# Attention on one core: another order of scores, products and normalisation in the steps, and other due times for the work beside them

## The chip, the core and the metric

One core of a Trainium2 chip runs the whole program. The metric is device time in microseconds of one execution; lower is better. Engines are called as the profile calls them: PE (TensorE, matmuls), PEld (its weight loads), DVE (VectorE), ACT (ScalarE), POOL (GpSimd), SP (SyncE, which issues the DMAs that matter here). Each works through its own instructions in order and waits on semaphores of the others.

## The reference

Three stages in a row: an attention, a dense layer pair with a rational activation, and eight experts of which each token takes one. The change lies in the first. Its mathematics, per batch (4), head (8), with 576 rows and 64 columns in float32:

```python
scores = (q @ k.T) / 8
thresh = scores.max(-1) - tau            # tau = 0.02
scores = where(scores >= thresh, scores, -1e9)
attn = exp(scores - scores.max(-1))
attn = attn / (attn.sum(-1) + 1e-9)
x = attn @ v
```

The result x, transposed and split into a float16 high and low part, is the input of the dense layers.

## The kernel before, in words

The attention (function `attention`, lines 161 to 631) handles two batches together (a batch pair, bp) and two heads together (a pair of heads, group g). A unit u is one head of a batch pair: nine tiles of 128 rows (t = 0 to 8), the middle one (t = 4) made of half a tile of each batch. There are N = 144 steps i, nine per unit, 18 per group, in eight groups; LAG = 12 more steps drain. The loop at line 596 writes out, for each step i, the instructions of all engines in this order:

- S(i+1), `emit_s`: the scores of the next tile, PE, float32, into one of three PSUM tiles of `ps_s` (line 377). q carries the factor -1/8, so the largest score is a minimum.
- the products with v of tile i - 12, `emit_pv` (lines 446 to 469): fourteen float16 matmuls of 65 columns with transposed weights `pt` and v in a high and a low part `vh`, `vl` (the 65th column, ones, gives the row sums). They add up in `xps`, a PSUM tile with two halves of three tiles of rows each; every third step a matmul of `tiny` (line 455; one row in 128 columns) starts a half.
- `emit_e`: the row's minimum (DVE, line 393) and the exponential (ACT, line 395) into a buffer e of four.
- `emit_thr`: minimum plus tau, by ACT or DVE as `THR` says (lines 402, 404).
- `emit_p(i-1)`: one DVE instruction compares with the threshold and multiplies (line 410), and is the last reader of that score tile; ACT rounds to float16 (line 419), POOL computes the remainder (lines 421, 422), and after every second step SP issues one transposing DMA from the ring `php` of four into `pt` (line 425). Steps from `DIRECT` = 138 on go through PE transposes (`emit_t`, line 431) instead.
- every third step, `emit_x`: reciprocal of the sums (line 486) and the multiply (line 488), both DVE, from the half of `xps` just finished into `xf`. In such a step S(i+1) is written behind the products.
- whatever `PLAN` has due at this step, through the dictionary `plan` filled by `at`. From step 112 on the next stage's generator `tail` advances too; its decoding of weights on DVE begins near step 144.

`PLAN` (line 138) gives steps within a group for the work beside the chain: loads of the next q and k (`load_qk`, SP), turning of q and k on PE in pieces of 16 matmuls or one (`piece_t`, line 244) and their copies by ACT (`piece_out`, lines 259 to 270), loads of v for the second batch pair (`load_v`), its sums (`sum_v1`), the split of v (`hi_v` on ACT, `lo_v` on POOL), and `emit_xt`: three PE transposes of `xf` (line 496), ACT's rounding to the high part of `xT` (line 498), DVE's low part (line 499). q, k and x share one PSUM bank, `tp`, for being turned. `FIRST` does the first group's q and k.

Of the kernel before, what the change touches and what calls it, by code (L numbers as in the profile page):

```python
# [18 lines left out]
P = 128  # L19
# [67 lines left out]
def plan_decode():  # L87
# [63 lines left out]
}  # L151
X_LAG = 0
THR = 'svvvsvvvv'
# [7 lines left out]
def attention(nc, tc, q, k, v, tau, xT, vs, ident, tail):  # L161
# [17 lines left out]
    e_p = pool(early, "e", 4)  # L179
# [20 lines left out]
    tiny = fix.tile([1, P + 3 * D1], BF16, name="tiny")  # L200
# [115 lines left out]
    def row_ps(bp, n):  # L316

        if bp == 0:
            return xps.rearrange("p a b c -> p (a b c)")[:, 2 * P + P * n:3 * P + n]
        return ps_x.tile([P, 4, P], F32, tag="tp", name="tp")[:, 0, 0:(P, 1)[n]]  # L320
# [23 lines left out]
    def hi_v(g, hh):  # L344
        bp, hp = divmod(g, 4)
        src = vall[:, hp, bp, hh, 0:8]
        nc.scalar.activation(vh[:, g % 2, hh, 0:8, 0:D], src, AF.Copy, scale=vs[:, bp, 0:1])
        if hh:
            nc.scalar.activation(last_v(g, vh), last_v(g), AF.Copy, scale=vs[:, bp, 0:1])

    def lo_v(g, a):
# [3 lines left out]
        parts = [(vall[:, hp, bp, hh, ts], *(x[:, g % 2, hh, ts, 0:D] for x in (vh, vl)))]  # L355
        if a == 3:
            last = last_v(g), last_v(g, vh), last_v(g, vl)
            parts += [tuple(x[:, :, h] for x in last) for h in range(2)] if g == 0 else [last]
# [113 lines left out]
    rs = [None]  # L472

    def emit_x(u, tg, part):
        xo = xps[:, (3 * u + tg) % 2]
        if part == 0:
            if tg == 0 and u % 2 == 0:
                xfs[u // 2] = x_p.tile([P, UT, 2, D], F32, tag="xf", name="xf")
            rs[0] = sm.tile([P, 3, 1], F32, tag="rinv", name="rinv")
            tot = xo[:, :, D:D1]  # L480
            i = u * UT + 3 * tg
            if i + 2 >= DIRECT:
                nc.vector.tensor_tensor(
                    rs[0], tot, sums[:, i - N + 3 * UT:i + 3 - N + 3 * UT].rearrange("p (a b) -> p a b", b=1), op=ALU.add)
                tot = rs[0]
            nc.vector.reciprocal(rs[0], tot)
        else:
            nc.vector.tensor_tensor(
                xfs[u // 2][:, 3 * tg:3 * tg + 3, u % 2], xo[:, :, 0:D], rs[0].to_broadcast([P, 3, D]), op=ALU.mult)

    def emit_xt(g, tg):
        bp, hp = divmod(g, 4)
        t0 = 3 * tg
        tp = ps_x.tile([P, 4, P], F32, tag="tp", name="tp")[:, 0:3]
        for t in range(3):
            nc.tensor.transpose(tp[:, t], xfs[g][:, t0 + t].rearrange("p h d -> p (h d)"), ident)
# [19 lines left out]
    nc.vector.memset(tiny[:, 0:P], 2.0**-15)  # L516
    nc.vector.memset(tiny[:, P:], 0.0)
    nc.vector.memset(tiny[:, P:].rearrange("p (a b) -> p a b", b=D1)[:, :, D:D1], 1e-9 * 2.0**15)
# [39 lines left out]
    for a in range(4):  # L558
# [9 lines left out]
    for g in range(1, NG):  # L568
        s0 = (g - 1) * GT
        o = 3 if g == 1 else 0  # L570
# [7 lines left out]
        for n in range(3):  # L578
            for i, (ts, outs) in ((1, ("k_t", "k_out")), (0, ("q_t", "q_out"))):
                at(s0 + o + PLAN[ts][n], piece_t, g, i, PIECES[n])  # L580
                for hh in range(2):
                    at(s0 + o + PLAN[outs][2 * n + hh], piece_out, g, i, *PIECES[n], (hh,))
        for hh in range(2):
            at(s0 + PLAN["v_hi"][hh], hi_v, g, hh)
        for a in range(4):
            at(s0 + PLAN["v_lo"][a], lo_v, g, a)
    x_lag = lambda u: X_LAG if u < NU - 1 else 0
# [1289 lines left out]
```

## Time and profile before

| | us |
|---|---|
| median of 3 runs | 1077.81 (1077.54 to 1080.48) |
| the profiled execution | 1076.23 |
| its span, first to last instruction | 1074.3 |
| mean granted clock of TensorE | 0.968 of 2.4 GHz |

Of the span the attention takes the first third: the first matmul of the dense layers starts at 356.91 us, in PE's order behind the last turned output. In rows of a timeline the columns are start, duration, engine, line, operation, tiles written and read, count, and in brackets how long the engine had been idle before it and what ended that. In rows of stretches they are the stretch, its length, the busy time and the instructions of each engine, the granted clock as a share of 2.4 GHz, the mean busy share of the DMA engines and their GB/s. In rows of groups: busy time in us, mean ns of one, then the idle time in front of them.

### The profile page before, as it was taken

How to read it: one execution, taken by the hardware profiler on the slowest of the kernel's cores; microseconds unless marked ns; L12 is line 12 of the kernel's file. 1: busy time of each engine (PE TensorE's matmuls, PEld its weight loads, DVE VectorE, ACT ScalarE, POOL GpSimd, SP SyncE). 2: the span in 40 equal slices, each digit the busy share in tenths (PEclk: the TensorE clock that was granted, in tenths of full speed). 3: DMA queues.
4: the chain of work that ended last, by engine and by line, in shares of the span. 5: the costliest groups of instructions: out<-in, count | busy, mean ns of one | idle time of the engine just before them, and what ended most of it. 6: DMA issues, size and time to landing. Idle time of an engine off the chain costs nothing. (4 is left out here: it accounts for less than half of the span.)

```text
span 1074.3 us, 19863 instructions
## 1 busy us (share of the span) xinstructions
PE 972.9 (91%) x7377; PEld 729.1 (68%) x7377; DVE 826.3 (77%) x1406; ACT 700.0 (65%) x1055; POOL 508.2 (47%) x547
## 2 busy tenths in 40 slices
PE   7999999999897688888899999998988999999996
PEld 5676676676666455555566666665557799999995
DVE  3987788788787579999897787899896697665552
ACT  4987897887775278777776656666564454554552
POOL 3687787788760254545555444443534013211120
PEclk8999999999997699999999999999899999999998
DMA  9799998998992213323200312204132111111340
GB/s 218 139 202 195 197 186 156 181 167 153 214 173 79 80 59 117 98 70 93 84 1 1 85 63 60 60 30 127 31 89 81 48 50 50 59 41 40 99 138 23
DMA packets 227176, 108.42 MB, mean 101 GB/s; under 512 B 189824, under 2 KB 214400, under 8 KB 227072
## 3 DMA queue, kind: packets, MB, share of 16 engines
q1 hardware_dynamic: 223808, 97.12, 41.0%
q0 software_dynamic: 3120, 9.96, 2.8%
q8 instruction: 60, 0.98, 0.4%
q14 instruction: 44, 0.36, 0.1%
q10 hardware_dynamic: 144, 0.00, 0.0%
HBM read 82.61 MB, written 13.63 MB: 90 GB/s over the span
## 5 line engine op out<-in xcount | busy, mean ns | idle before, releaser
L939 PE MATMUL h<-xT,wih 128*128 128x384 f16 x768 | 194.3, 336 | 44.1 <-DVE s L956 31.8
L966 POOL TENSOR_TENSOR t<-t,ah 128x768 f32<-128x768 f32 x48 | 87.8, 1828 | 229.5 <-ACT t L965 214.7
L421 POOL TENSOR_TENSOR php<-e,php 128x512 f16<-128x512 f32 x138 | 160.3, 1162 | 73.0 <-ACT php L419 72.9
L377 PE MATMUL s<-kt,qz 128*128 128x288 f32 (+1 forms) x640 | 172.2, 426 | 13.4 <-DVE e L410 10.0
L939 PEld LDWEIGHTS <-wih 128*128 128x128 f16 x768 | 69.9, 100 | 110.6 <-DVE s L956 39.1
L395 ACT ACTIVATE e<-s,mn 128x576 f32<-128x576 f32 x144 | 106.5, 739 | 58.4 <-DVE mn L393 44.7
L1009 PE MATMUL acc<-woh,gh 128*128 128x512 f32 x288 | 126.5, 439 | 4.2 <-ACT part L1026 1.8
L939 PE MATMUL h<-xT,wil 128*128 128x384 f16 x384 | 128.4, 334 | 0.5 <-POOL wil L858 0.5
L377 PEld LDWEIGHTS s<-kt,qz 128*128 128x128 f32 (+1 forms) x640 | 99.0, 181 | 41.5 <-DVE e L410 13.2
L393 DVE TENSOR_REDUCE mn<-s 128x1 f32<-128x576 f32 x144 | 108.0, 750 | 24.6 <-PE s L377 24.3
L410 DVE SCALAR_TENSOR_TENSOR e<-s,mn,e 128x576 f32<-128x576 f32 x144 | 116.5, 809 | 5.4 <-ACT e L395 4.1
L1009 PE MATMUL acc<-wol,gh 128*128 128x512 f32 x288 | 114.9, 399 | 2.6 <-POOL wol L864 2.6
L1009 PE MATMUL acc<-woh,gl 128*128 128x512 f32 x288 | 114.4, 397 | 0.0
L1705 POOL DMA_INDIRECT out_dram<-os,sidx x19 | 23.8, 1253 | 182.2 <-ACT os L1704 152.9
L991 POOL TENSOR_TENSOR gl<-s,gh 128x768 fp32r<-128x768 f32 x48 | 91.3, 1903 | 6.9 <-issue 4.6
L419 ACT ACTIVATE php<-e 128x576 f16<-128x576 f32 x138 | 93.7, 679 | 0.2
L469 PEld LDWEIGHTS <-pt 128*128 128x128 f16 (+1 forms) x2142 | 76.4, 101 | 19.3 <-issue 9.2
L469 PE MATMUL xps<-vs__112,pt 128*128 128x65 f16 (+1 forms) x2142 | 86.4, 195 | 0.0
L963 ACT ACTIVATE ah<-h,cvs 128x768 f32<-128x768 f32 x48 | 43.3, 902 | 53.6 <-PE h L939 50.0
L975 ACT ACTIVATE h<-t,co 128x768 f32<-128x768 f32 x48 | 43.4, 905 | 52.1 <-DVE s L969 18.6
L1638 DVE TENSOR_TENSOR wol<-xT,woh 128x1024 fp32r<-128x1024 f32 x45 | 56.8, 1270 | 17.0 <-ACT woh L1637 17.0
L1009 PEld LDWEIGHTS acc<-woh,gh 128*128 128x128 f32 x288 | 54.8, 190 | 20.6 <-ACT part L1026 4.7
(401 smaller groups left out, 2341.7 us busy)
## 6 DMA issues: line engine op xcount, KB each, us to landing
xT<-in_moe_w_dram SPq DMA_DIRECT2D x80, 512.0 KB
raw<-in_moe_w_in_dram SPq DMA_DIRECT2D x16, 512.0 KB
raw<-in_moe_w_out_dram SPq DMA_DIRECT2D x16, 512.0 KB
yd<-y SPq DMA_DIRECT2D x18, 256.0 KB
raw<-in_k_dram SPq DMA_DIRECT2D x16, 256.0 KB
raw<-in_q_dram SPq DMA_DIRECT2D x16, 256.0 KB
xT<-in_v_dram SPq DMA_DIRECT2D x8, 512.0 KB
part<-part SPq DMA_DIRECT2D x15, 256.0 KB
```

Source lines behind the costliest of these rows:

```text
L377: nc.tensor.matmul(ps[po:po + m, half, 0:288], qz[:, g % 2, hh, t, qt:qt + m], kt[:, c:c + 288], start=True, stop=True)
L393: nc.vector.tensor_reduce(mn[:, 0:1], ps[:, :, 0:288], axis=AX.XY, op=ALU.min)
L395: nc.scalar.activation(e, ps[:, :, 0:288], AF.Exp, bias=mn[:, 0:1], scale=-1.0)
L410: nc.vector.scalar_tensor_tensor(e, ps[:, :, 0:288], mn[:, 1:2], e, op0=ALU.is_le, op1=ALU.mult, accum_out=sums[:, i - N + 3 * UT:][:, 0:1 ...
L419: nc.scalar.activation(ph.rearrange("p (a b) -> p a b", a=2), e, AF.Copy)
L421: nc.gpsimd.tensor_tensor(pl[:, 64:S], ef[:, 0:512], ph[:, 0:512], op=ALU.subtract)
L469: nc.tensor.matmul(x, w, y, start=False, stop=(t % 3 == 2 and n == len(seq) - 1))
L939: nc.tensor.matmul(hb[:, 0:n], w[:, k, fc * P:(fc + 1) * P], xT[:, k, t0:t0 + TR, lo, :], start=(i == 0), stop=(i == 11))
L966: nc.gpsimd.tensor_tensor(t1, t1, ah, op=ALU.mult)
L991: nc.gpsimd.tensor_tensor(gl, s, gh.bitcast(F32), op=ALU.subtract)
L1009: nc.tensor.matmul(acc[r, i], g[:, i * P:(i + 1) * P], w, start=first and m == 0, stop=last and m == 2)
L1638: (self.nc.gpsimd if pool else self.nc.vector).tensor_tensor(cut(lo), src, cut(hi).bitcast(F32), op=ALU.subtract)
```

## The change

In the loop, S(i+1) is written ahead of the products with v in every step. `emit_x` is one function for both of its parts; it is due one step later than before, three steps being those of a half of `xps`, and stands at the head of its step, ahead of the products, the minimum and the rest (in the very last step behind them). `emit_xt` keeps the transposes and the high part; the low part becomes `emit_xlo`, due one step later. The due times in `PLAN` change: pieces of k at steps -2, 0, 2 of a group, of q at 4, 6, 8, turned output at 10, 12, 14 (28, 30, 32 counted from its own group's start), copies of a piece at the step after it and both halves together; for the second group these come six steps later (`late`) where it was three. The loads of v for the second batch pair come at 14, 20, 26, 32 instead of 12, 20, 28, 40; the low parts of v in five steps instead of four, the last high part in a step of its own. The threshold is always DVE's. The buffers e become five. `tiny` has 128 rows, zero but for the first. The sums' row in the second batch pair uses a tile of `ps_s` instead of `tp`.

```diff
 PLAN = {
-    "k_load": (7, 9),
-    "q_load": (14, 16),
-    "k_t": (-1, 3, 4),
-    "k_out": (0, 1, 3, 3, 5, 6),
-    "q_t": (7, 10, 11),
-    "q_out": (8, 9, 10, 10, 12, 13),
-    "v_hi": (15, 17),
-    "v_lo": (15, 17, 19, 20),
+    "k_load": (4, 6),
+    "q_load": (10, 12),
+    "k_t": (-2, 0, 2),
+    "q_t": (4, 6, 8),
+    "late": 6,
+    "v_hi": (11, 13, 15),
+    "v_lo": (14, 17, 20, 23, 25),
     "v_first": (2, 7, 8),
-    "v_next": (12, 20, 28, 40),
-    "v_sum": (24, 29, 42, 60, 61, 62, 68, 69),
-    "xt": (32, 33, 34),
+    "v_next": (14, 20, 26, 32),
+    "v_sum": (25, 31, 37, 43, 45, 46, 48, 49),
+    "xt": (28, 30, 32),
 }
-THR = 'svvvsvvvv'
+THR = 'v'
-    e_p = pool(early, "e", 4)
+    e_p = pool(early, "e", 5)
-    tiny = fix.tile([1, P + 3 * D1], BF16, name="tiny")
+    tiny = fix.tile([P, P + 3 * D1], BF16, name="tiny")
...
     def emit_xt(g, tg):
...
-        hi, lo = (xT[:, hp, bp * UT + t0:bp * UT + t0 + 3, n] for n in range(2))
-        nc.scalar.activation(hi, tp, AF.Copy)
-        nc.vector.tensor_tensor(lo, tp, hi, op=ALU.subtract)
+        nc.scalar.activation(x_rows(g, tg, 0), tp, AF.Copy)
+        xts[g, tg] = tp
+
+    def emit_xlo(g, tg):
+        nc.vector.tensor_tensor(x_rows(g, tg, 1), xts.pop((g, tg)), x_rows(g, tg, 0), op=ALU.subtract)
...
-        o = 3 if g == 1 else 0
+        o = PLAN["late"] if g == 1 else 0
...
-            pre[u * UT + 3 * tg + 2 + LAG + x_lag(u)] = (u, tg)
+            pre[min(u * UT + 3 * tg + 3 + LAG, N + LAG - 1)] = (u, tg)
...
-        if i + 1 < N and not early_pv:
+        if i + 1 < N:
             emit_s(i + 1)
+        done = i in pre and i < N + LAG - 1
+        if done:
+            emit_x(*pre[i])
         if 0 <= i - LAG < N:
             emit_pv(i - LAG)
...
-        if i + 1 < N and early_pv:
-            emit_s(i + 1)
         if i < N:
             emit_e(i)
-        if i < N and THR[i % len(THR)] != "v":
-            emit_thr(i)
         if 0 <= i - 1 < N:
             emit_p(i - 1)
...
-        if last:
-            emit_x(*pre[i], 0)
-        if i < N and THR[i % len(THR)] == "v":
+        if i in pre and not done:
+            emit_x(*pre[i])
+        if i < N:
             emit_thr(i)
-        if last:
-            emit_x(*pre[i], 1)
```

## Rows read from the trace of the kernel before

**Rows 1.** The page's part 1: each engine's busy time over the span.
```profile
PE 972.9 (91%) x7377; PEld 729.1 (68%) x7377; DVE 826.3 (77%) x1406; ACT 700.0 (65%) x1055; POOL 508.2 (47%) x547
```
**Rows 2.** Stretches: six groups of 18 steps, from S(17) to S(125).
```profile
51.11:88.29 37.18, 35.67 (x445) 26.05 (x441) 30.48 (x63) 32.27 (x59) 30.76 (x46) 1.00 1.11 202
...
243.74:282.30 38.56, 36.23 (x442) 26.67 (x442) 31.42 (x66) 30.73 (x57) 30.77 (x46) 1.00 0.93 163
sum 231.19, PE 217.35 PEld 159.67 DVE 188.60 ACT 188.57 POOL 184.74; mean PE 36.23 PEld 26.61 DVE 31.43 ACT 31.43 POOL 30.79
```
**Rows 3.** Stretches: S(3) to S(6); S(125), S(139), S(143); the drain.
```profile
14.86:28.11 13.25, 8.53 (x63) 6.11 (x62) 6.04 (x10) 6.51 (x12) 3.98 (x6) 0.74 0.97 210
...
282.30:310.45 28.15, 25.76 (x292) 18.29 (x292) 23.95 (x52) 21.33 (x38) 24.28 (x37) 0.94 1.07 212
310.45:321.93 11.48, 9.39 (x100) 6.86 (x99) 7.93 (x20) 7.27 (x15) 3.56 (x6) 1.00 0.86 162
321.93:336.00 14.07, 9.15 (x152) 7.67 (x152) 11.12 (x31) 7.79 (x18) 0.00 (x0) 0.92 0.22 74
336.00:356.91 20.91, 18.88 (x84) 16.09 (x84) 11.73 (x33) 7.14 (x14) 2.38 (x2) 0.50 0.34 102
```
**Rows 4.** Timeline, all engines, around a step that turns output.
```profile
240.73 1.14 PE L377 MATMUL s<-kt,qz 128*128 128x288 f32 x4
...
241.74 0.56 DVE L499 TENSOR_TENSOR xT<-tp,xT 128x384 f16<-128x384 f32 x1 [1.09 <-ACT xT L498]
...
241.79 0.25 PE L455 MATMUL xps<-tiny 1*128 1x195 bf16 x1
...
241.98 0.60 PE L469 MATMUL xps<-vs__112,pt 128*128 128x65 f16 x14
242.21 0.75 DVE L393 TENSOR_REDUCE mn<-s 128x1 f32<-128x576 f32 x1
...
242.43 0.52 PE L496 MATMUL tp<-ident,xf 128*128 128x128 f32 x3
...
242.87 0.81 DVE L410 SCALAR_TENSOR_TENSOR e<-s,mn,e 128x576 f32<-128x576 f32 x1
...
243.74 1.24 PE L377 MATMUL s<-kt,qz 128*128 128x288 f32 x4 [0.79 <-DVE e L410]
```
**Rows 5.** Groups by line and form, 40 to 330 us: DVE's instructions of a step.
```profile
L410 DVE SCALAR_TENSOR_TENSOR e<-s,mn,e 128x576 f32<-128x576 f32 x135 | 109.3, 809 | 5.4 <-ACT e L395 4.1 <-ACT mn L402 0.6
L393 DVE TENSOR_REDUCE mn<-s 128x1 f32<-128x576 f32 x134 | 100.5, 750 | 13.9 <-PE s L377 13.8
...
L404 DVE TENSOR_SCALAR mn<-mn,tauc 128x1 f32<-128x1 f32 x105 | 20.5, 195 | 0.0
...
L488 DVE TENSOR_TENSOR xf<-xps,rinv 128x192 f32<-128x192 f32 x44 | 15.7, 357 | 0.0
...
L499 DVE TENSOR_TENSOR xT<-tp,xT 128x384 f16<-128x384 f32 x21 | 11.7, 557 | 28.1 <-ACT xT L498 28.1
...
L486 DVE RECIPROCAL rinv<-xps 128x3 f32<-128x3 f32 x44 | 7.6, 173 | 5.6 <-PE xps L469 5.6
```
**Rows 6.** Timeline, drain: DVE's multiply and the next matmul into xps.
```profile
330.67 0.36 DVE L488 TENSOR_TENSOR xf<-xps,rinv 128x192 f32<-128x192 f32 x1
...
331.08 0.24 PE L455 MATMUL xps<-tiny 1*128 1x195 bf16 x1 [1.00 <-DVE xf L488]
```
**Rows 7.** Timeline, start: the second group's first piece of k on PE.
```profile
22.29 1.97 PE L244 MATMUL tp<-ident,raw 128*64 128x128 f32 x16 [4.72 <-DMA raw<-in_k_dram]
```
**Rows 8.** Waits, 51.11 to 321.93 us: total, times, longest.
```profile
ACT e L395 <- POOL php L422: 12.6, 11, 2.1
```
**Rows 9.** Timeline, SP's queue: first, one between and the one after ten transposes.
```profile
57.12 2.74 SPq L425 DMA_TRANSPOSE pt<-php  x1
...
65.75 3.25 SPq L425 DMA_TRANSPOSE pt<-php  x1
...
101.40 3.31 SPq L425 DMA_TRANSPOSE pt<-php  x1
```

More of the change, by code (lines that the diff above doesn't have):

```diff
@@ L319, in row_ps @@
             return xps.rearrange("p a b c -> p (a b c)")[:, 2 * P + P * n:3 * P + n]
-        return ps_x.tile([P, 4, P], F32, tag="tp", name="tp")[:, 0, 0:(P, 1)[n]]
+        return ps_s.tile([P, 2, 512], F32, tag="s", name="s")[:, 0, 0:(P, 1)[n]]
     def red_row(bp):
@@ L354, in lo_v @@
         ts = slice(4 * half, 4 + 4 * half)
-        parts = [(vall[:, hp, bp, hh, ts], *(x[:, g % 2, hh, ts, 0:D] for x in (vh, vl)))]
-        if a == 3:
+        if a < 4:
+            parts = [(vall[:, hp, bp, hh, ts], *(x[:, g % 2, hh, ts, 0:D] for x in (vh, vl)))]
+        else:
             last = last_v(g), last_v(g, vh), last_v(g, vl)
-            parts += [tuple(x[:, :, h] for x in last) for h in range(2)] if g == 0 else [last]
+            parts = [tuple(x[:, :, h] for x in last) for h in range(2)] if g == 0 else [last]
         for src, hi, lo in parts:
@@ L471, in attention, with emit_x @@
     xfs = {}
-    rs = [None]
-    def emit_x(u, tg, part):
+    def emit_x(u, tg):
         xo = xps[:, (3 * u + tg) % 2]
[L476 to L487, printed above, removed]
-            nc.vector.tensor_tensor(
-                xfs[u // 2][:, 3 * tg:3 * tg + 3, u % 2], xo[:, :, 0:D], rs[0].to_broadcast([P, 3, D]), op=ALU.mult)
+        if tg == 0 and u % 2 == 0:
+            xfs[u // 2] = x_p.tile([P, UT, 2, D], F32, tag="xf", name="xf")
+        rs = sm.tile([P, 3, 1], F32, tag="rinv", name="rinv")
+        tot = xo[:, :, D:D1]
+        i = u * UT + 3 * tg
+        if i + 2 >= DIRECT:
+            nc.vector.tensor_tensor(
+                rs, tot, sums[:, i - N + 3 * UT:i + 3 - N + 3 * UT].rearrange("p (a b) -> p a b", b=1), op=ALU.add)
+            tot = rs
+        nc.vector.reciprocal(rs, tot)
+        nc.vector.tensor_tensor(
+            xfs[u // 2][:, 3 * tg:3 * tg + 3, u % 2], xo[:, :, 0:D], rs.to_broadcast([P, 3, D]), op=ALU.mult)
@@ L491, in emit_xt, with x_rows @@
+    def x_rows(g, tg, n):
+        bp, hp = divmod(g, 4)
+        t0 = bp * UT + 3 * tg
+        return xT[:, hp, t0:t0 + 3, n]
+    xts = {}
     def emit_xt(g, tg):
-        bp, hp = divmod(g, 4)
-        t0 = 3 * tg
         tp = ps_x.tile([P, 4, P], F32, tag="tp", name="tp")[:, 0:3]
         for t in range(3):
-            nc.tensor.transpose(tp[:, t], xfs[g][:, t0 + t].rearrange("p h d -> p (h d)"), ident)
-        hi, lo = (xT[:, hp, bp * UT + t0:bp * UT + t0 + 3, n] for n in range(2))
-        nc.scalar.activation(hi, tp, AF.Copy)
@@ L515, in attention @@
     nc.vector.memset(sums, 0.0)
-    nc.vector.memset(tiny[:, 0:P], 2.0**-15)
-    nc.vector.memset(tiny[:, P:], 0.0)
-    nc.vector.memset(tiny[:, P:].rearrange("p (a b) -> p a b", b=D1)[:, :, D:D1], 1e-9 * 2.0**15)
+    nc.vector.memset(tiny, 0.0)
+    nc.vector.memset(tiny[0:1, 0:P], 2.0**-15)
+    nc.vector.memset(tiny[0:1, P:].rearrange("p (a b) -> p a b", b=D1)[:, :, D:D1], 1e-9 * 2.0**15)
     nc.vector.memset(vl[:, :, :, :, D:D1], 0.0)
@@ L557, in attention @@
         at(PLAN["v_first"][1] + hh, hi_v, 0, hh)
-    for a in range(4):
+    at(PLAN["v_first"][1] + 1, hi_last, 0)
+    for a in range(5):
         at(PLAN["v_first"][2] + a // 2, lo_v, 0, a)
@@ L596, in attention @@
     while i < N + LAG or plan:
-        last = i in pre
-        early_pv = last and x_lag(pre[i][0]) == 0
         if DIRECT <= i - 2 < N - 1:
             emit_t(i - 2)
-        if i + 1 < N and not early_pv:
+        if i + 1 < N:
             emit_s(i + 1)
+        done = i in pre and i < N + LAG - 1
+        if done:
+            emit_x(*pre[i])
         if 0 <= i - LAG < N:
```

19 lines of the change are left out of this document (10 added, 9 removed).

## The prediction, written before the result was known

> **What bounds the kernel now.** I read the page's engine line first, then busy time by stretch, then one group's timeline, then durations by line. TensorE is busy 91% of the span [rows 1], but that is a mean over stages, and the change touches only the attention (start to 356.91 us) and its hand-over. So I cut the attention at starts of S, the scores' matmul, 18 steps (one pair of heads) apart: S(17) at 51.11, S(35) at 88.29 and so on to S(125) at 282.30. There are six such groups; the first, the last and the sum stand in [rows 2]. Read two columns: 231.19 us in all, PE busy 217.35. PE is the bound, yet idle for 13.84 us; DVE is busy 188.60, ACT 188.57, POOL 184.74, so none of them is a second bound on average. Nothing that keeps the same matmuls can win more than 13.84 us there. The other stretches [rows 3] are the start, where S(3) to S(6) take 13.25 us with PE busy 8.53; the last pair's steps (28.15 and 11.48 us with PE busy 25.76 and 9.39); and the drain from S(143), of which 336.00 to 356.91 runs at a granted clock of 0.50, the 1.2 GHz level.
>
> Where PE's idle time is made shows in [rows 4], a step that turns output for the next stage. DVE waited 1.09 us for ACT's rounding (L498) before it could write the low part (L499, 241.74). The next minimum (L393) is ready but stands behind it on DVE, then the product with the threshold (L410), and only that frees the score bank: S at 243.74 waited 0.79 us for it. S, minimum, exp, rounding, low part and S again run one after the other, with three such steps in a row in each group.
>
> **The change, part by part.**
>
> Turned output. The low part moves one step on, and the turns go from three consecutive steps to every second one. One L499 costs 0.557 us [rows 5] before and after; its wait goes, since ACT has rounded a step earlier. What is late next is PE itself, or the bank turn below.
>
> Output normalised one step on, S always ahead of the products with v. The reciprocal and the multiply (L486, L488) now stand ahead of the next minimum on DVE, and behind the end of the third product. Both halves of xps belong to one tile, and the trace shows them ordered against each other: the matmul of tiny into the other half began at 331.08, 0.05 us after the multiply (330.67 + 0.36) ended [rows 6]. So behind a waiting reciprocal are queued: the next minimum, the product L410, and through it S two steps on, and on PE the next products. From the end of the products: reciprocal and multiply 0.53 [rows 5], minimum to product 0.66, product 0.81 [rows 4, 5], and about 0.1 for the hand-overs, 2.1 us to the S that needs the bank. PE has meanwhile S 1.06, tiny 0.19 and the products 0.45 (starts 240.73, 241.79, 241.98, 242.43) [rows 4], 1.70 us, and any transposes placed in those two steps. Uncovered: 0.4 us for a turn without transposes. Of six turns a group, two have only a small tail transpose (about 0.14 us of cover), the other four a whole piece, turned output or the doubled scores of a middle tile. I put 0.55 us a group on turns and 0.25 on other short waits: 0.8 x 6 = 4.8 left of the 13.84, a gain of 9.0 us. Bounds: 13.84, and 3 if every turn loses 0.3 (36 x 0.3 = 10.8).
>
> The Trainium skill's page "PSUM — Partial Sum Buffer", section "PSUM bank collisions raise a hardware error", speaks against this move: accesses of two engines must be kept apart by bank and quadrant, not by address, so the second half doesn't let PE go on while DVE reads the first. The order at 331.08 agrees. By it tiny waits 0.55 us behind the turn, which the 1.06 us of S hides; by address alone it would wait for nothing, and the sum would be the same.
>
> Threshold always on DVE: four more a group at 0.195 [rows 5] make 0.8 us on a DVE busy 31.4 of 38.5 us [rows 2]; hidden, and ACT gets a little back. If DVE were the bound it would cost 5 us in all.
>
> Start. The first piece of the second pair's k is turned at step 4 in place of 2. PE, in order, waited 4.72 us for that load at 22.29 [rows 7], with S(4) to S(6) queued behind it; that is most of the 4.7 us of idle PE before S(6) [rows 3]. Two steps later, S(4), S(5) and the warming matmuls fill the wait: the piece still starts at 22.29, runs about 1.1, and S(6) starts near 23.4 in place of 28.11. Gain 4.7; at worst 2 if ACT's sums of v are next in line, at best 7, since the 0.74 clock of this stretch would rise with a fuller PE.
>
> Last pair. No q or k pieces are left to cover turns here. In 28.15 us PE is busy 25.76 at 0.94 clock; I give back about 1 us for the clock and take three uncovered turns of 0.4: 26.5, a gain of 1.6. In the 11.48 us after it, three turns of output with the wait of [rows 4] meet PE transposes of e; PE needs 9.39 [rows 3]; gain 2. Together 3.6, from 1 to 6.
>
> Drain. The decoding of weights on DVE is not changed. The normalisation now stands behind a step's decoding on DVE and can hold PE at three turns; PE's idle time just before 336, 14.07 less 9.15, bounds that at some +4. In return the low part's wait no longer blocks decoding. Were the clock to stay at 2.4 GHz, PE's 18.88 us from 336 would halve, and DVE's 11.73 [rows 3] would be the floor: -8. PE is as thinly used before it as now (9.15 of 14.07 us), so I take 0.
>
> tiny over 128 rows. 0.19 us from its start to the products' now; 195 columns at the pace of the products (0.45 / 14 for 65) take 0.10. Saves between 0 and 0.09 x 47 = 4.2; a load of 128 rows might cost 0.5 instead. I take 2, since the new form is the products' own.
>
> Fifth e buffer, low parts of v in five steps, both halves of a piece in one step: instruction counts stay; ACT's 12.6 us of waits for POOL [rows 8] lie beside a PE that is busy. Nothing. Without that cover it would be part of the 13.84 already counted.
>
> DMA. The loads of v for the second batch pair move from steps 12 to 40 into 14 to 32, on SP's queue among the transposes of the weights. In 57.12 to 101.40 this queue never rested: ten transposes with six loads of q or k and two of v in 44.28 us [rows 9]. A transpose alone takes 3.2 of the queue [rows 9], so 12 us are loads: about 1.1 for one of 256 KB and 2.7 for one of v with its tail. Steps 14 to 34 will ask for 10 x 3.2 + 6 x 1.1 + 4 x 2.7 = 49 us where PE needs 41. Eight us of lateness is about what the four-deep ring of php absorbs; I take +1, from 0 to +5.
>
> Sum: -4.7 - 9.0 - 3.6 + 0 - 2 + 1 = -18.3. The profiled execution took 1076.23 (span 1074.3), 1.6 below the median of 1077.81; set against the median it is 1059.5, against the execution 1057.9. I say **1059**.
>
> **Rivals.**
> - *The turn of the bank is the new wait.* DVE's order is for it, TensorE's cover against. If all 36 turns lose 0.4, 14.4 us replace the 13.84: no gain in the groups, 1068. Chance 0.14.
> - *The clock holds in the drain*: for it a denser end of the scores, against it the unchanged decoding. -8: 1051 and below. Chance 0.12.
> - *Slower: SP's queue sets the pace.* If lateness passes what ring and lag absorb, ACT waits to write php, and the chain runs at the queue's 4.43 us a pair. From S(17) to S(139), 61 pairs, 270 us against 259.3 now: +11, less 4.7 and 2 at both ends, +4: 1082. It decides if transposes start over some 8 us behind POOL beyond step 34. Against: after it a group asks only 9 x 3.2 + 4 x 1.1 = 33 us. The Trainium skill's page "DMA: Bandwidth & Descriptors", section "Issuing engines are not separate DMA queues", says that all issuers share the same sixteen engines; the busy queue here agrees, and no other queue would take these loads off. Chance 0.10.
> - *It does not do what it says*: one wait takes another's place on the same banks, and what the start gains is lost in the drain: 1075 to 1080. Chance 0.07.
>
> **How the numbers follow.** Forecast (1051 to 1067) 0.57. 0.3%, or 3.2 us, is about what a measurement here tells from no change. Faster 0.57 + 0.14 + 0.12 = 0.83, within 0.07, slower 0.10. The range takes in the clock's and the bank turn's cases, 1046 to 1073, and leaves out 0.17 and the last tails.
>
> **What would show it.** Right: waits of L499 for L498 near zero, S(17) near 46, groups of about 37 us with PE busy 36, S(6) near 23.4. The turn: S waiting for L410 in steps just behind a reciprocal. The queue: transposes starting 8 us behind POOL, ACT waiting at L419. Wrong at large: groups over 38.5 us, or a half-clock stretch longer than now.

## The result, and the profile after

The changed kernel takes 1065.6 us in the median of 7 runs (1062.79 to 1073.14), the kernel before 1077.81 (1077.12 to 1080.48): a ratio of 0.989 [0.986, 0.993], or 12.2 us less. The forecast was 1059 in a range of 1046 to 1073. The profiled execution took 1072.34 (span 1070.6), which is near the upper end of its seven. Nothing below rests on its total alone: the same kernel was profiled again (e1_again), and that execution took 1064.31.

Busy time by stretch of the kernel after, cut at the same starts of S as [rows 2] and [rows 3] (columns: stretch, its length, busy time and count on PE, PE's weight loads, DVE, ACT and POOL, granted clock, DMA share, GB/s): start to S(6), to S(17), the first three groups, the last group, the last pair's two pieces, the drain, and all that follows the attention.

```profile
0.00:23.77 23.77, 18.82 (x153) 13.37 (x153) 13.76 (x31) 13.45 (x22) 10.13 (x16) 1.00 1.00 224
23.77:46.49 22.72, 21.62 (x191) 15.49 (x189) 19.65 (x47) 19.59 (x34) 13.69 (x21) 1.00 0.88 157
46.49:83.63 37.14, 35.20 (x448) 27.12 (x444) 31.57 (x69) 32.98 (x57) 30.65 (x47) 1.00 1.08 205
83.63:128.49 44.86, 38.92 (x445) 29.29 (x446) 33.28 (x77) 34.10 (x59) 31.82 (x48) 0.92 1.09 200
128.49:164.78 36.29, 35.16 (x442) 27.12 (x442) 32.10 (x70) 30.45 (x52) 31.03 (x47) 1.00 1.00 172
...
237.34:273.62 36.28, 35.16 (x441) 27.13 (x442) 32.09 (x70) 30.45 (x52) 31.03 (x47) 1.00 1.09 184
273.62:299.29 25.67, 23.57 (x292) 18.07 (x292) 24.09 (x52) 19.47 (x31) 24.96 (x39) 1.00 1.20 216
299.29:311.12 11.83, 9.31 (x102) 6.80 (x99) 9.80 (x26) 6.78 (x15) 3.09 (x5) 1.00 0.83 155
311.12:344.74 33.62, 26.19 (x233) 22.97 (x233) 21.26 (x58) 14.09 (x31) 2.67 (x2) 0.67 0.31 95
344.74:1070.60 725.86, 654.21 (x3766) 492.51 (x3764) 555.96 (x807) 434.49 (x576) 267.36 (x191) 0.97 0.21 64
```

Set beside before: S(17) is 4.6 us earlier; the six groups take 227.1 in place of 231.19 (the last four 36.28 to 36.29 each, the last of them 38.56 before [rows 2], but the second 44.86); the last pair's 37.50 stands against 39.63, the drain's 33.62 against 34.98 [rows 3]. That makes 4.6 + 4.1 + 2.1 + 1.4 = 12.2 us, and the attention indeed ends at 344.74 in place of 356.91. Behind it this execution gave 8.5 us back (725.86 against 1074.3 - 356.91 = 717.39), at a mean granted clock of 0.97.

Two places carry the story. First the second group, which has a hole: a stretch in which the chain stands still. One wait of ACT in it (total, times, longest):

```profile
ACT php L419 <- DMA pt<-php: 4.6, 2, 4.1
```

The rows around the hole, each from its own engine's timeline (start, length, engine, line, what; in brackets the idle time before it and what ended it): POOL's end of one pair of php, the DMA transpose of this pair on SP's queue (its length there is that of the issue, not of the transfer), ACT's next write into the same buffer, and PE.

```profile
88.31 0.31 POOL L422 TENSOR_TENSOR php<-e,php 128x64 f16<-128x64 f32 x1
...
95.34 4.33 SPq L425 DMA_TRANSPOSE pt<-php  x1
...
103.27 0.68 ACT L419 ACTIVATE php<-e 128x576 f16<-128x576 f32 x1 [4.11 <-DMA pt<-php]
103.86 1.36 ACT L264 ACTIVATE qz<-tp,tauc 64x512 f32<-64x512 f32 x2
...
101.54 0.60 PE L469 MATMUL xps<-vs__112,pt 128*128 128x65 f16 x14
105.28 0.48 PE L237 MATMUL tp<-ident,tail 128*128 128x128 f32 x1 [3.14 <-ACT qz L264]
```

POOL had finished this pair at 88.62. SP's queue came to its transpose only at 95.34, 6.7 us late, and by the trace's semaphores the transpose landed at 103.19, 7.85 us after its start. Four pairs on, the ring of php comes round to the same buffer: ACT's write, ready 4.11 us earlier, began at 103.27. Behind it on ACT stood the copy of turned q (L264) that frees the tile of turns, and for that PE stood still from 102.14 to 105.28. From 104.4 to 111.2 the granted clock was at its lower level, 1.2 GHz, which is why the group's mean clock is 0.92.

The second place is a turn of the output bank in the last groups. Timeline, PE and DVE, around one reciprocal:

```profile
205.08 0.60 PE L469 MATMUL xps<-vs__112,pt 128*128 128x65 f16 x14
...
205.52 1.21 PE L377 MATMUL s<-kt,qz 128*128 128x288 f32 x4
205.72 0.18 DVE L483 RECIPROCAL rinv<-xps 128x3 f32<-128x3 f32 x1 [1.20 <-PE xps L469]
205.93 0.36 DVE L484 TENSOR_TENSOR xf<-xps,rinv 128x192 f32<-128x192 f32 x1
206.21 0.75 DVE L393 TENSOR_REDUCE mn<-s 128x1 f32<-128x576 f32 x1
...
206.57 0.25 PE L455 MATMUL xps<-tiny 128*128 128x195 bf16 x1
...
206.87 0.81 DVE L410 SCALAR_TENSOR_TENSOR e<-s,mn,e 128x576 f32<-128x576 f32 x1
...
207.74 1.24 PE L377 MATMUL s<-kt,qz 128*128 128x288 f32 x4 [0.34 <-DVE e L410]
```

DVE stood idle for 1.20 us until the products (L469) ended and it could take the reciprocal. From there the chain is the one of the forecast: 205.72 to 207.68 on DVE, and S waits 0.34 for the product L410 (0.4 was forecast). The wait of [rows 4], the low part behind ACT's rounding, is gone from these groups. PE's waits in the last four groups are small, and the first is of this kind:

```profile
PE s L377 <- DVE e L410: 2.7, 8, 0.3
PE s L377 <- DVE mn L404: 1.3, 4, 0.3
```

The second is not: the same row, 1.3 us in 4 waits, stands in the four such groups of e12_v_step34, where the reciprocal has its old place. What is in doubt is whether the reciprocal ought to stand at the head of its step at all.

### The profile page after: what moved, and what is told of

Its sections match the earlier page's. It is cut to its first block, busy times and chain, and to the rows that moved or that the text cites. A ratio compares the mean times of both kernels' runs of the same rounds, so it can differ in the third digit from the quotient of the medians.

```text
span 1070.6 us, 19851 instructions
## 1 busy us (share of the span) xinstructions
PE 968.5 (90%) x7377; PEld 734.1 (69%) x7377; DVE 837.7 (78%) x1438; ACT 696.7 (65%) x1023; POOL 508.5 (47%) x547
## 5 line engine op out<-in xcount | busy, mean ns | idle before, releaser
L939 PE MATMUL h<-xT,wih 128*128 128x384 f16 x768 | 197.3, 340 | 47.1 <-DVE s L956 32.3
L966 POOL TENSOR_TENSOR t<-t,ah 128x768 f32<-128x768 f32 x48 | 87.7, 1827 | 235.2 <-ACT t L965 219.9
L377 PE MATMUL s<-kt,qz 128*128 128x288 f32 (+1 forms) x640 | 176.5, 428 | 12.7 <-DVE mn L404 5.0
L410 DVE SCALAR_TENSOR_TENSOR e<-s,mn,e 128x576 f32<-128x576 f32 x144 | 116.3, 808 | 7.9 <-ACT e L395 7.8
L469 PEld LDWEIGHTS <-pt 128*128 128x128 f16 (+1 forms) x2142 | 82.4, 101 | 27.9 <-issue 9.2
L469 PE MATMUL xps<-vs__112,pt 128*128 128x65 f16 (+1 forms) x2142 | 88.4, 195 | 0.0
```

The source lines that it names most:

```text
L377: nc.tensor.matmul(ps[po:po + m, half, 0:288], qz[:, g % 2, hh, t, qt:qt + m], kt[:, c:c + 288], start=True, stop=True)
L410: nc.vector.scalar_tensor_tensor(e, ps[:, :, 0:288], mn[:, 1:2], e, op0=ALU.is_le, op1=ALU.mult, accum_out=sums[:, i - N + 3 * UT:][:, 0:1 ...
L469: nc.tensor.matmul(x, w, y, start=False, stop=(t % 3 == 2 and n == len(seq) - 1))
L939: nc.tensor.matmul(hb[:, 0:n], w[:, k, fc * P:(fc + 1) * P], xT[:, k, t0:t0 + TR, lo, :], start=(i == 0), stop=(i == 11))
L966: nc.gpsimd.tensor_tensor(t1, t1, ah, op=ALU.mult)
```

## The experiments

Each of the twelve runs stood beside the kernel before on the same chip; the medians of before lay between 1077.8 and 1080.3, so the ratio is what is compared. The columns "last group" and "six groups" are lengths in the profiled execution, "attention" is when its last product with v has made way for the first dense matmul.

| run | what differs | median us | ratio to before | last group | six groups | attention |
|---|---|---|---|---|---|---|
| before | | 1077.81 | 1 | 38.56 | 231.2 | 356.9 |
| after | the change | 1065.6 | 0.989 [0.986, 0.993] | 36.28 | 227.1 | 344.7 |
| e1_again | nothing | 1067.3 | 0.990 [0.989, 0.992] | 36.29 | 225.0 | 344.5 |
| e2_spread | loads of v later | 1058.57 | 0.982 [0.981, 0.984] | 36.28 | 219.1 | 336.3 |
| e3_lo_same | e2, low part in the step of its turn | 1095.99 | 1.019 [1.016, 1.021] | 40.77 | 248.5 | 372.3 |
| e4_tiny1 | e2, tiny on one row | 1062.62 | 0.985 [0.984, 0.987] | 36.39 | 219.9 | 338.7 |
| e5_x_old | e2, output normalised as before | 1054.3 | 0.976 [0.974, 0.977] | 34.78 | 216.8 | 332.7 |
| e6_late4 | e2, second pair's pieces two steps earlier | 1066.92 | 0.988 [0.986, 0.990] | 36.29 | 220.3 | 342.6 |
| e7_drain | e2, drain normalised earlier | 1060.3 | 0.982 [0.980, 0.983] | 36.28 | 219.7 | 337.8 |
| e8_warm | e2, more matmuls in the drain | 1059.67 | 0.981 [0.979, 0.983] | 36.29 | 219.5 | 339.1 |
| e9_before_lo | before, low part one step on | 1063.49 | 0.985 [0.982, 0.988] | 35.60 | 221.2 | 341.2 |
| e10_v_early3 | e5, v at 5, 8, 11, 44 | 1055.36 | 0.979 [0.977, 0.982] | 34.78 | 218.1 | 333.5 |
| e11_v_early4 | e5, v at 5, 8, 11, 14 | 1054.93 | 0.977 [0.974, 0.979] | 34.78 | 216.4 | 332.2 |
| e12_v_step34 | e5, v at 5, 8, 11, 34 | 1047.43 | 0.972 [0.970, 0.974] | 34.78 | 210.5 | 328.0 |

**e1_again: the change, unaltered.**

> The changed kernel once more, for a second profile. Its seven runs scattered from 1062.8 to 1073.1; its profile (1072.3) had one group of 18 steps, S(35) to S(53), of 44.9 us where the later ones take 36.3, with ACT waiting 4.6 us for a transposing DMA. Theory Q (SP's queue is late once, and by how much differs from run to run): 1063 to 1073 again; a run near 1063 has that group at 37 to 40 us, one near 1072 at 44 or more. Rival C (the clock in the dense stages makes the scatter): that group is 44 to 45 us in any run, and fast and slow runs differ only behind 360 us.

The hole is there again: S(35) to S(53) took 42.91 us, the four groups behind it 36.28 to 36.29 each, and the attention ended at 344.5. What follows the attention took 718.00, against 725.86 in the first profile and 717.39 before:

```profile
85.24:128.15 42.91, 36.29 (x445) 27.61 (x446) 33.23 (x77) 34.15 (x59) 31.80 (x48) 1.00 1.06 208
...
344.50:1062.50 718.00, 648.39 (x3766) 489.23 (x3764) 553.46 (x807) 434.53 (x576) 267.77 (x191) 0.98 0.22 65
```

So the hole belongs to the kernel, nearer to rival C than to theory Q, while the 8.5 us given back behind the attention belong to that execution. Here PE stood still for 2.09 us in the hole, the clock did not fall (1.00), and the group was 1.95 us shorter than in the first profile. Behind the attention the clock stood at the 1.2 GHz level for 34 us here, 49 in the first profile and 37 before; why it stood there longer in one execution of the same kernel was not settled.

**e2_spread: the four loads of v where before had them.**

```diff
-    "v_next": (14, 20, 26, 32),
-    "v_sum": (25, 31, 37, 43, 45, 46, 48, 49),
+    "v_next": (12, 20, 28, 40),
+    "v_sum": (25, 31, 37, 52, 53, 54, 56, 57),
```

> The changed kernel with one thing undone: the loads of v for the second batch pair at steps 12, 20, 28, 40 as before the change (their sums by step 57 instead of 49). Theory Q: no wait of ACT for a transposing DMA, S(35) to S(53) in 37 us, transposes at most 5 us behind POOL; 1060 to 1063, scatter under 4 us. Rival C: that group stays above 42 us and the time at 1063 to 1073.

Busy time by stretch, the second to the fourth group:

```profile
82.32:118.85 36.53, 35.24 (x441) 27.13 (x442) 32.21 (x70) 31.90 (x55) 31.81 (x48) 1.00 1.11 213
118.85:156.26 37.41, 36.21 (x445) 27.63 (x446) 32.78 (x77) 32.45 (x56) 31.10 (x47) 1.00 1.09 193
156.26:192.55 36.29, 35.17 (x441) 27.13 (x442) 32.10 (x70) 30.45 (x52) 31.02 (x47) 1.00 1.07 188
```

The second group fell from 44.86 (42.91 in e1_again) to 36.53, the ratio from 0.990 to 0.982, some 8.5 us. The sums of v move with the loads, so some of the second group's work now stands in the third, 37.41 in place of 36.29; over the first three groups 118.29 (116.09 in e1_again) became 110.23, a hole of 5.9 to 8.1 us. Up to S(71) transposes start up to 6.8 us late here too, but none of them lands after ACT wants its buffer back, and ACT waits for no transpose: theory Q as to the cause. Every further edit but e9_before_lo stands on this kernel.

**e3_lo_same: the low part again in the step of its turn.**

```diff
-            at(min(s0 + 1, N + LAG - 1), emit_xlo, g, tg)
+            at(s0, emit_xlo, g, tg)
```

> As e2_spread, but the low part of the turned output in the same step as its high part. If DVE's wait for ACT is what the late low part saves: waits of the low part for the high part back at 15 to 25 us in all, groups of 36.3 become 38 to 39, +10 to +15 us over e2_spread. If two steps for each bank alone do it, the wait returns but lies beside PE work: groups at most 36.8, within 3 us of e2_spread.

One group by stretch, then DVE's waits from 46 to 273 us:

```profile
213.72:254.49 40.77, 35.05 (x442) 27.16 (x442) 32.15 (x70) 30.47 (x52) 31.09 (x46) 1.00 0.85 158
```

```profile
DVE rinv L483 <- PE xps L469: 23.1, 22, 3.1
DVE xT L502 <- ACT xT L498: 21.9, 15, 2.3
```

and PE's longest, from 46 to 330 us (4.1 in e2_spread):

```profile
PE s L377 <- DVE mn L404: 28.0, 23, 1.8
```

It costs 37 us over e2_spread, more than twice what was expected. In this order DVE waits twice, for PE's products and for ACT's rounding, S waits for DVE, and a group takes 40.77 with PE no busier than in e2_spread. The kernel is then slower than before: the rest of the change without the late low part would have lost.

**e4_tiny1: tiny with one row.**

```diff
-    tiny = fix.tile([P, P + 3 * D1], BF16, name="tiny")
+    tiny = fix.tile([1, P + 3 * D1], BF16, name="tiny")
```

> As e2_spread, but tiny with one row as before the change. PE takes 0.19 instead of 0.08 us from a start of tiny to the products behind it. If PE is the bound at every turn: 0.11 x 47, +5 us, groups of 36.9. If the turn's wait for DVE hides it: within 1 us.

```profile
194.10:230.49 36.39, 36.00 (x441) 26.79 (x442) 32.15 (x70) 30.43 (x52) 30.99 (x47) 1.00 0.92 174
```

The median rose by 4.0, near the 5 of the first case, but a group took 36.39 and not 36.9. The attention ended 2.4 later; 0.7 of this was there at S(6), before any matmul of tiny, and 1.5 came from S(17) on. The row is worth a second look: PE's busy time went from 35.16 to 36.00, the group's length only from 36.28 to 36.39. Busy time of PE and time are not the same thing here, to which the section on the prediction comes back.

**e5_x_old: the output normalised in the step of its third product, as before.** S follows the products in these three steps of a unit, as it did before.

```diff
-            pre[min(u * UT + 3 * tg + 3 + LAG, N + LAG - 1)] = (u, tg)
+            pre[u * UT + 3 * tg + 2 + LAG] = (u, tg)
...
-        if i + 1 < N:
+        done = i in pre
+        if i + 1 < N and not done:
             emit_s(i + 1)
-        done = i in pre and i < N + LAG - 1
-        if done:
-            emit_x(*pre[i])
         if 0 <= i - LAG < N:
             emit_pv(i - LAG)
...
+        if i + 1 < N and done:
+            emit_s(i + 1)
...
-        if i in pre and not done:
+        if done:
             emit_x(*pre[i])
```

> The version with spread loads (e2_spread, 1058.57 us), with one part undone: the output is again normalised in the step of its third product, behind that product, and in these steps S again follows the products. The low part stays one step on. Theory A (normalising one step on, with S always ahead, is a second cause of the filled groups): PE waits for the bank turn again, groups of 38 to 39 us in place of 36.28, attention ends at 346 to 353 in place of 336.3, time 1068 to 1074. Theory B (the late low part alone fills the groups): groups of 36.3 to 36.8, time 1057 to 1061.

One group, the second group and the drain:

```profile
81.28:121.30 40.02, 35.93 (x441) 27.73 (x442) 32.23 (x70) 31.93 (x55) 31.80 (x48) 0.96 1.11 203
...
193.45:228.24 34.79, 34.46 (x442) 26.62 (x442) 32.06 (x70) 30.52 (x52) 30.93 (x47) 1.00 0.97 178
...
300.36:332.65 32.29, 26.20 (x232) 22.98 (x233) 20.41 (x58) 14.06 (x31) 2.31 (x2) 0.69 0.32 98
```

Neither theory: A had undoing the part cost 10 us and more, B had it change nothing, and it gains 1.5 us a group (34.78 in place of 36.28); the ratio falls to 0.976. Normalising one step on, with S ahead, costs. Of the 1.5, about 0.7 is less busy PE and the rest less idle PE. With the shorter groups the queue was late again in the second (40.02), where ACT's writes of php waited 4.3 us for transposes.

**e6_late4: the first piece of the second pair's k at step 2 again.** The other pieces of this pair, and the next pair's loads, move two steps forward with it.

```diff
-    "late": 6,
+    "late": 4,
```

> e2_spread with the first piece of the second pair's k turned at step 4 + -2 = 2, where the kernel before turned it, in place of step 4. Theory A (the start's gain is S(4) to S(6) no longer standing behind a transpose that waits for its load): S(6) goes from 23.3 back to about 28, everything behind it keeps its distances, time 1062 to 1064. Theory B (the start gains by the order of v's sums and scalings, not by this step): S(6) stays within 1 us of 23.3, time 1058 to 1060.

Start to S(6); in e2_spread this took 23.30:

```profile
0.00:27.90 27.90, 20.05 (x153) 14.52 (x154) 11.57 (x28) 12.64 (x20) 8.99 (x14) 0.94 0.94 210
```

S(6) went back to 27.90, 4.6 later, as theory A has it, with PE waiting 4.6 us for that load of k (1.7 in e2_spread). The attention ends 6.3 later, the ratio is 0.006 higher: the start's gain reaches the end, and a little more.

**e7_drain: in the drain, the output normalised in the step of its last product.**

```diff
-            pre[min(u * UT + 3 * tg + 3 + LAG, N + LAG - 1)] = (u, tg)
+            e = u * UT + 3 * tg + 2 + LAG
+            pre[e if e >= N - 1 else e + 1] = (u, tg)
...
-        done = i in pre and i < N + LAG - 1
+        done = i in pre and i < N - 1
```

> e2_spread with one change behind the scores: in the drain the output is normalised in the step of its last product, ahead of the next decoding on DVE, in place of one step on. In the drain of e2_spread PE waited some 2 to 3 us twice for the multiply L484, which stood behind decoding. Theory A (these waits are PE's): they go, the drain's 33.64 us become 29 to 31, time 1054 to 1056. Theory B (PE and DVE share the drain, what PE gains is lost by the later decoding): drain within 1 us of 33.64, time 1057.5 to 1060.

PE's waits in the drain, of the kernel after first, then of this one, and last its stretch:

```profile
PE xps L455 <- DVE xf L484: 5.6, 3, 2.8
```

```profile
PE xps L455 <- DVE xf L484: 2.6, 3, 1.1
PE h L823 <- ACT wih L814: 1.9, 1, 1.9
```

```profile
305.48:337.76 32.28, 26.19 (x232) 22.97 (x233) 20.41 (x58) 14.01 (x31) 2.31 (x2) 0.69 0.32 98
```

In e2_spread the first wait was 4.8. Of the 2.2 us taken from it 1.9 came back as the wait of a small matmul of the next stage (L823) for ACT's rounding of its decoded weights (L814); the drain is 1.4 shorter, the median not (ratio 0.982, as e2_spread). That is between the theories in the drain's length and theory B in the time, by the wait that took the other's place.

**e8_warm: twelve more small matmuls, whose results nobody reads, in each of the first six steps of the drain.**

```diff
+        if N <= i < N + 6:
+            warm(ps_x.tile([P, 4, P], F32, tag="tp", name="tp").rearrange("p a b -> p (a b)"), 12)
```

> e2_spread with twelve more small matmuls, whose results nobody reads, in each of the first six steps of the drain, to keep PE busier there. In e2_spread the granted clock was at 0.50 from 311 us for 27 us, in the drain. Theory A (the thin use of PE makes the clock fall, and the low clock is what the drain costs): the stretch at 0.50 in the drain is gone or under 12 us, the drain is 26 to 29 us in place of 33.64, time 1051 to 1055. Theory B (DVE's decoding bounds the drain at either clock): the clock stays, the drain is within 1.5 us, time 1057 to 1060. Theory C (the added matmuls stand in front of waiting products): drain of 35 to 38 us, time 1060 to 1064.

The drain, of e2_spread first, then of this one:

```profile
302.64:336.28 33.64, 27.29 (x233) 24.16 (x234) 21.28 (x58) 14.04 (x31) 2.67 (x2) 0.63 0.30 94
```

```profile
305.44:339.15 33.71, 29.70 (x305) 26.54 (x306) 21.77 (x58) 14.08 (x31) 2.65 (x2) 0.83 0.30 95
```

Its last part, from the start of the last half of xps, again of e2_spread first:

```profile
326.09:336.28 10.19, 9.24 (x40) 8.43 (x40) 3.65 (x10) 1.04 (x2) 0.00 (x0) 0.50 0.33 99
```

```profile
328.92:339.15 10.23, 9.28 (x40) 8.47 (x40) 3.94 (x10) 1.10 (x3) 0.29 (x1) 0.50 0.34 103
```

The mean granted clock rose from 0.63 to 0.83, and the drain took 33.71 in place of 33.64: the clock as theory A has it, the length as theory B. This does not show what the clock is worth in the drain. In the first 23.5 us, where the clock rose from 0.69 to 0.97, the added matmuls themselves took PE six times 1.47 us, and what came last was the multiply behind DVE's decoding. The last 10.2 us stood at 0.50 in both, with PE busy for nine tenths of them.

**e9_before_lo: the kernel before with the late low part alone.** The row of v's scale moves to a score bank and one piece of k turns a step later, so that the one tile for turns is free.

```diff
-    "k_t": (-1, 3, 4),
-    "k_out": (0, 1, 3, 3, 5, 6),
+    "k_t": (0, 3, 4),
+    "k_out": (1, 2, 3, 3, 5, 6),
...
         nc.scalar.activation(hi, tp, AF.Copy)
-        nc.vector.tensor_tensor(lo, tp, hi, op=ALU.subtract)
+        xts[g, tg] = tp, hi, lo
...
+    def emit_xlo(g, tg):
+        tp, hi, lo = xts.pop((g, tg))
+        nc.vector.tensor_tensor(lo, tp, hi, op=ALU.subtract)
...
             at(s0, emit_xt, g, tg)
+            at(min(s0 + 1, N + LAG - 1), emit_xlo, g, tg)
```

> The kernel before with one part of the change alone: the low part of turned output (the old L499) moves one step on. To keep one tile for the turns, the first piece of k is turned one step later (0 in place of -1), and the row of v's scale goes to a score bank. The turns stay in three consecutive steps, and normalising, order of S and products, tiny, v stay as before. Theory A (the wait of the low part alone is what kept PE idle): groups of 35.3 to 36.8 in place of 37.2 to 40.4, ratio to before 0.985 to 0.991. Theory B (turns in consecutive steps still wait, now for the low part of the turn before, so that the spread to every second step is needed too): groups of 37.5 to 39, ratio 0.994 to 1.002.

The third group, the last group and the last pair:

```profile
121.96:164.43 42.47, 38.29 (x447) 27.84 (x446) 32.70 (x73) 34.38 (x61) 32.45 (x49) 0.96 1.09 197
...
235.62:271.22 35.60, 35.30 (x443) 26.54 (x442) 31.51 (x66) 30.67 (x56) 30.69 (x47) 1.00 0.99 185
271.22:295.48 24.26, 23.96 (x293) 17.32 (x291) 23.26 (x51) 20.12 (x35) 23.38 (x36) 1.00 1.12 216
```

Theory A in five of the six groups, 35.6 to 36.1. The low part brings the last group from 38.56 [rows 2] to 35.60, with PE busy 35.30 of it, and the last pair's first piece from 28.15 [rows 3] to 24.26; the four steps behind that piece stay at 11.49. The ratio, 0.985, is already that of the whole change or below; 1.0 us of it is S(17) at 50.07, which the piece of k moved by a step can have won. One group has a hole of its own (42.47), with a write of php that waited 2.9 us for a transpose.

**e10_v_early3, e11_v_early4, e12_v_step34: where the loads of v belong.** In e5_x_old the transposes start on time up to the sixth, the queue resting some 2 us a pair; then they run late, by 9.2 us at worst. The three runs move three or four of the loads into the start.

```diff
-    "v_next": (12, 20, 28, 40),
+    "v_next": (5, 8, 11, 44),
```

> e5_x_old (normalisation in the old step, spread loads, 1054.3 us at ratio 0.9756) with three of the four loads of v for the second batch pair issued at steps 5, 8 and 11 in place of 12, 20 and 28, and the last at 44 in place of 40. In e5_x_old the transposes start on time up to pair 5 (43.28 us), the queue resting 2 us a pair, and are late from pair 6 on, by 9.2 us at pair 15; S(35) to S(53) took 40.03 us and S(53) to S(71) 37.37 in place of 34.78. Theory A (the lateness is that of SP's queue, and loads in its resting time cost nothing): both groups fall to 34.8 to 35.5, time down by 6 to 8: ratio 0.968 to 0.970. Theory B (early loads take from the loads of the start, or of the second group's k): S(6) or S(17) come 2 to 6 us later, ratio 0.972 to 0.977.

> As e10_v_early3, with the fourth load of v at step 14 in place of 44. Theory A (a load in the start's slack is free, later ones cost the queue): as e10_v_early3 within 2 us, S(53) to S(71) lower by up to 2 us. Theory B (from S(17) on the queue has no slack, and this load falls where it starts to fill): S(35) to S(53) longer by 2 to 4 us than in e10_v_early3.

Of e10_v_early3, SP's queue and ACT's timeline around its hole; of e11_v_early4, PE's waits from 46 to 88 us:

```profile
109.63 0.57 SPq L277 DMA_DIRECT2D xT<-in_v_dram  x1
...
114.54 0.49 ACT L498 ACTIVATE xT<-tp 128x384 f16<-128x384 f32 x1 [6.97 <-DMA xT<-in_v_dram]
```

```profile
PE tp L242 <- DMA raw<-in_q_dram: 3.3, 1, 3.3
```

e10_v_early3 is neither theory: its transposes start at most 2 us late up to the hole, and the start is not longer (S(17) at 45.95), but S(35) to S(53) took 42.61, since ACT's write of turned output into xT stood 6.97 us behind a load of v into the same tile (into its other half), which the queue issued only at 109.63, two us after ACT had come to wait for it (114.54 - 6.97 = 107.57). In e11_v_early4 that load went early as well, and now the queue was late in the first group: q's load came late, PE waited 3.3 us for it, and S(17) to S(35) took 40.88 in place of 35.03, while S(35) to S(53) fell to 35.11. The time is theory A's, the lateness theory B's, one group earlier than it said. The last run puts the load into the gap between both:

> As e10_v_early3, with the last load of v issued at step 34 in place of 44. In e10_v_early3 the transposes start on time up to pair 20, so the queue is no longer late, and S(35) to S(53) is long (42.61) for another reason: ACT's write of turned output into xT (L498, step 46) waited 6.97 us for the load of v into xT that was issued at 109.63 us. Theory A (that one wait is the rest): issued twelve steps ahead of the write, the load has landed; S(35) to S(53) falls to 34.8 to 36.5, time down by 6 to 8 against e10_v_early3, ratio 0.971 to 0.974. Theory B (any place for the fourth load makes the queue late): transposes start over 5 us behind POOL between pairs 14 and 20, S(35) to S(53) of 38 to 41, ratio 0.976 to 0.979.

```profile
82.86:117.96 35.10, 34.52 (x441) 26.60 (x442) 32.10 (x70) 31.74 (x55) 31.68 (x48) 1.00 1.12 194
117.96:154.01 36.05, 35.23 (x445) 27.04 (x446) 32.83 (x77) 32.13 (x56) 30.87 (x47) 1.00 1.09 190
154.01:188.79 34.78, 34.45 (x441) 26.61 (x442) 32.05 (x70) 30.51 (x52) 30.96 (x47) 1.00 1.10 198
```

Theory A: no hole is left (transposes start up to 5.1 us late, and no write waits for one), the six groups take 210.5 us, and the median is 1047.43, a ratio of 0.972 [0.970, 0.974]. This beats both kernels: it is the change without its second part (the output normalised as before), with three loads of v in the start's slack and the fourth at step 34.

## Why the prediction was right or wrong

The sign and the range came out, the size to two thirds (12.2 of 18.3 us), and that partly by errors that cancel: the term for the DMAs was 5 to 7 us too kind, a part of what was to win 9.0 in the groups costs 8.6, and the late low part is worth more than the ceiling that the forecast gave it. With the queue out of the way (e2_spread) the attention ends 20.6 us earlier, where the forecast's terms without the DMAs make 19.3.

**Start, -4.7: right.** S(6) at 23.77 (23.4 forecast), S(17) at 46.49 (near 46). e6_late4 takes back the two steps and S(6) goes back to 27.90. The filling is not complete, as the forecast had it: PE still waited 2.23 us for the load before the piece began at 22.74. In e1_again S(17) came at 48.4: S(6) to S(17) took 24.41 at a mean clock of 0.93, against 22.72 at 1.00, so this gain itself varies by some 2 us from run to run.

**Groups, -9.0: the size held where the queue let it, the ceiling and the division among the parts did not.** Four groups took 36.28 to 36.29, better than the forecast's 37. In e2_spread, with the queue out of the way, the six gain 12.1; with the output normalised as before and no holes (e12_v_step34) they gain 20.7. That is above the 13.84 which the forecast called the most there is. The step that failed is "Nothing that keeps the same matmuls can win more than 13.84 us there": it took PE's busy time of [rows 2] for a floor. e9_before_lo keeps every matmul, and its last group is 2.96 us shorter where PE had been idle for 2.33: PE's busy time itself fell, from 36.23 to 35.30. Between e4_tiny1 and e2_spread 0.84 of busy time went with 0.11 of time. So PE's busy time here is no floor; that the recorded matmuls contain waiting which goes when their neighbours move is the likely reading, not a shown one. The Trainium skill's page "Perfetto Trace Analysis", section "Identifying the Most-Contended Engine", warns of this measure: matmul busy time is not a good gauge of how close TensorE is to its limit, because pipelined instructions look smaller in the trace. The runs agree that it is no good gauge; whether the matmuls look smaller or larger than they are, they do not show.

**Which part carries the gain.** The forecast put the low part and the normalisation into one term, "late next is PE itself, or the bank turn". The runs part them. The late low part alone (e9_before_lo) takes 3.0 us from the last group, and in the new order, where DVE also waits for the products, 4.5 (e3_lo_same against e2_spread). Normalising one step on with S always ahead takes nothing away: it adds 1.5 a group (e2_spread against e5_x_old), 8.6 us over the six (219.1 against 210.5 in e12_v_step34, both without a hole). The forecast had the mechanism and its price for a turn: 0.4 uncovered, 0.34 measured, and 0.7 us a group of PE waiting for L410 in the rows of the kernel after, in two turns of six, where it said 0.55. But it set this against a ceiling of idle time as what remains of a gain, and never asked what the old place of the reciprocal would cost once the low part was out of the way. That question was open in [rows 5]: the reciprocal's wait there was 5.6 us over 44 instructions, the low part's 28.1 over 21. What the rest of the change does for a group (turns at every second step, all thresholds on DVE, the fifth buffer e, tiny) was not parted further; together it is the 0.8 us between the 35.60 of e9_before_lo and the 34.78 of e5_x_old.

As to the Trainium skill's page "PSUM — Partial Sum Buffer", section "PSUM bank collisions raise a hardware error", which the forecast weighed: tiny at 206.57 began 0.28 behind the end of the multiply (206.29), with S in between, so the rule by bank and the row agree. It cost nothing, as said.

**DMA, +1 with bounds 0 to +5: the step that failed.** The lateness was forecast well: eight us by the sum, and the transposes of the hole start 6.7 and 7.2 us late. (The split of the queue behind it was off: of the 44.28 us of [rows 9] the ten transposes held 36.2 and the loads 8.1, where the forecast had 32 and 12.) That this "is about what the four-deep ring of php absorbs" was not priced from a row. From POOL's end of the pair to ACT's next need of its buffer were 10.5 us in this trace, and the transpose itself took 7.85 us from its start to its landing (4.6 to 8.3 for others of these groups): 6.7 + 7.85 is 4 us too many. The pair before, 5.9 late, cost ACT 0.45. And behind ACT on the same engine stood PE's next operand. The hole cost 5.9 to 8.1 us over the first three groups, of which 3.14 is PE's visible wait in the longer case; that one has the 6.8 us at the clock's lower level, the other has not. The medians say the same (0.990 against 0.982). The rival *SP's queue sets the pace* named this mechanism and its point, eight us; it failed in having it last for all 61 pairs. Behind the four loads the queue caught up, and the next groups ran at 36.29. That no other queue would take these loads off was not tested.

**Last pair, -3.6: 2.1.** 25.67 for its first piece, better than 26.5. The four steps behind it took 11.83 and not 9.5: S there waits for ACT's copies of turned e (L443), which the change does not touch, 2.5 us in all in e2_spread and 1.2 before. The forecast gave the gain to the wait of [rows 4], which was not what ended last there: in e9_before_lo, with the late low part alone, the four steps take 11.49 as before.

**Drain, 0 with bounds -8 and +4: the sum is -1.4.** PE waited 5.6 us for the multiply behind the decoding, as the forecast feared; that the decoding started freer in return was not shown. e7_drain takes part of that wait away and meets the decoding instead. The rival *the clock holds in the drain* did not come: the clock fell there as before, to a mean of 0.67. What it would be worth stays open. e8_warm raised the clock only in the first 23.5 us, and there by matmuls that took PE's time; the same eight products with v that took 1.86 us at the 1.2 GHz level took 1.03 there, and the last 10.2 us, where PE is busy nearly throughout, were not reached.

**tiny, -2: about right.** e4_tiny1 costs 1.5 us from S(17) to the attention's end and 4.0 by the median, with 0 to 4.2 as bounds. Only 0.1 of a group's 36.28 is of it.

**The bank turn's rival, 1068.** Its price for a turn was measured, but only 8 of 24 turns of the last four groups paid it, and its time was not reached, since the low part's wait was worth more than the ceiling. "It does not do what it says" fell with the last four groups.

## What to carry to other kernels

When a change bundles two moves that share an engine's queue, price each against the other already done: here one move won 3 to 4.5 us a group and hid that the second lost 1.5. When a ring of buffers is to absorb a queue's lateness, price it for one buffer: the lateness plus the transfer's own time to its landing, against the time until the writer comes round; what is over is a hole as soon as anything stands behind the writer on its engine. And place extra loads in the stretch where the queue is seen to rest between transposes, well ahead of any write to the same tile.

## What the runs showed of the hardware that was not expected

- The granted clock in the drain could be raised from a mean of 0.63 to 0.83 by matmuls whose results nobody reads, and the stretch took 33.71 us against 33.64; its last 10.2 us stayed at 0.50 in both.
- A transpose started on SP's queue landed 4.6 to 8.3 us later in the first two groups of the kernel after, where its issue held the queue for 2.4 to 4.6 us.
- One-row tiny counted 0.84 us more of busy PE in a group and 0.11 us more of time.
- PE stood still for 3.14 us in the hole of the first profile, and the clock was at the 1.2 GHz level from 104.4 to 111.2; in e1_again it stood still for 2.09 us at the same place, and the clock stayed at 2.4 GHz.
- What follows the attention took 717.39, 718.00, 719.89 and 725.86 us (before, e1_again, e2_spread, the first profile of the kernel after) with the same instructions there; the granted clock of that stretch was 0.98, 0.98, 0.98 and 0.97. e4_tiny1 had 725.73. What decides it stays open.
